# Pair 8 of an attention block sums its exponentials on VectorE too, and a weight conversion and one tile's transposes move forward

## The chip, the cores and the metric

The kernel runs on one core of a Trainium2 chip. The metric is the device time of one execution in microseconds (us); the runs of the kernel before have a median of 508.8 us (508.6 to 509.04). The engines are named as in the profile: PE is TensorE (matmuls), DVE is VectorE, ACT is ScalarE, POOL is GpSimd, SP is the engine that issues the transfers. Lines such as L415 are lines of the kernel before unless said otherwise.

## The reference, cut to what matters

All arrays are float32 but for the weights, which are float64.

```
attn:  s = (q @ k.T) / 8 ; s = 30 * tanh(s / 30) ; p = exp(s - max)      # 2 batches, 12 heads, 448 x 64
       out = (p / (sum(p) + 1e-9)) @ v
x   =  out laid out as 896 tokens x 768
moe:   h = x @ w_in                     # 768 -> 1024
       e = exp(h - max) ; solu = h * e / (sum(e) + 1e-9)
       ln = (solu - mean) / sqrt(var + 1e-6) * g_ln
       y = ln @ w_out                   # 1024 -> 768
moe2:  (sigmoid(y @ w_gate) * (y @ w_val)) @ w_out        # 768 -> 1536 -> 768
```

## The kernel before, in words

Four stages follow each other, and PE, ACT, DVE and POOL each run their instructions in the order in which the code issues them (a manual order holds for those four up to the end of the second matrix product; SP's transfers and what follows are placed by the scheduler).

**Attention.** The 24 heads are 12 pairs. A pair takes two slots (u = 0 and 1), each with half of the keys. In slot s, `s_mm` (L192) multiplies the scores of the next half on PE, `s_tanh` (L198) and `s_exp` (L220) work on ACT, and `s_pv` multiplies the exponentials of this slot with v (L238) and with a column of ones to get the row sums. For most pairs the sums come from the exponentials themselves: four matmuls in each of the two slots (L246). For the pairs in `ADD_PAIRS`, DVE first adds the two key blocks of each head (`es`, L232), in either slot, and four matmuls (L244) at the end of the second slot read the four added tiles. Pair 8 is in slots 16 and 17, pair 9 in 18 and 19. From slot 16 on the first matrix product (L405) of the first two token tiles is worked in beside attention: at the end of slot 16 `x_split` cuts tile 0 of x into a high and a low part (ACT L391, DVE `xl` L392), and at the end of slot 17 the first 12 of that tile's 36 matmuls stand.

**First product, tiles 2 to 6.** Tokens are in seven tiles of 128. A loop over t runs the 36 matmuls of tile t, then the transposes of tile t - 1 (`ln_trans`, L449, 8 on PE). On DVE stand `ln_max` (L415, after the tile's last matmul), `ln_he` (L423, after ACT's exponential L420), `ln_stats` (L429 to L434, then POOL L435), `ln_evac` of tile t - 1 (ACT L455 writes `lnhi`, then DVE L456 writes `lnlo`) and the first line of `ln_norm` (L439), after which ACT normalises the tile (L441).

**Weight conversion.** The float64 weights of the second product come as 12 chunks, two for each of its six column blocks. A chunk has six steps, which are in a list `todo`: A on ACT (L347), B, C and D on DVE (L352, L353, L354), E on DVE and ACT (L355, L334, then the cast L336 that gives the high part), F on DVE (L339, the low part). `fill(n)` issues the next n steps of the list where it stands in the code. The chunks overlap in the list: from chunk 3 on each group of six reads F of chunk c - 2, E of c - 1, B, C, D of c, A of c + 1. Five steps are issued in attention; before, the loop over t issues four for each of five tiles, 20 in all.

**Second product.** `l2(m, g)` makes column block m for token group g (tiles 0 to 2, or 3 to 6): 24 matmuls (L634) into one of two PSUM buffers (`pso`, tag `o`), then the evacuation of the block before (`y_evac`: ACT L648 writes `y_hi`, DVE L649 writes `y_lo`), then `fill(4)`. The order is (0, 0), (1, 0), the transposes and evacuation of tile 6, then (0, 1), (1, 1) and the rest. The third block, (0, 1), writes the PSUM buffer of the first, and reads the parts of tile 6. Third and fourth product follow.

Of the kernel before, what the change touches and what calls it, by code (L numbers as in the profile page):

```python
# [43 lines left out]
AHEAD = 3  # L44
W2_BUFS = 9

ADD_PAIRS = range(9, 11)

L1_BESIDE = 2
S_L1 = 16  # L50
# [22 lines left out]
def f32(ap):  # L73
    return ap.bitcast(F32)
# [7 lines left out]
def fused_kernel(ctx: ExitStack, tc: tile.TileContext, qk, v, cap, w_in, w_mid, g_ln, w_gv, w_fin, outT):  # L82
# [53 lines left out]
    with tc.If(bounded > 0) as cmp:  # L136
        network(tc, sh, False, w_in, w_mid, w_gv, w_fin, outT)
    with cmp.Else():
        network(tc, sh, True, w_in, w_mid, w_gv, w_fin, outT)
# [3 lines left out]
def network(ctx: ExitStack, tc: tile.TileContext, sh, general, w_in, w_mid, w_gv, w_fin, outT):  # L143
# [5 lines left out]
    def big():  # L149
        t = ps.tile([P, 2, 512], F32, tag="big", name="big")  # L150
        return t
# [70 lines left out]
    def s_pv(i, u):  # L222
# [4 lines left out]
        e = [es.pop((2 * i + j, u)) for j in range(2)]  # L227
        add = i in ADD_PAIRS and not general
        if add:
# [74 lines left out]
    def fill(k):  # L304
        for _ in range(min(k, len(todo))):
            todo.popleft()()
# [76 lines left out]
    def x_split(t, eng=nc.vector):  # L383
        xh = lin2.tile([P, K1, P], F32R, tag="xh", name="xh")
        xl = lin2.tile([P, K1, P], F32R, tag="xl", name="xl")
        t0 = t * P
        for b in range(B):
            lo, hi_ = max(t0, b * S), min(t0 + P, (b + 1) * S)
            if lo < hi_:
                src = x_sb[b][:, :, lo - b * S:hi_ - b * S]  # L390
                nc.scalar.copy(xh[:, :, lo - t0:hi_ - t0], src)  # L391
                eng.tensor_tensor(xl[:, :, lo - t0:hi_ - t0], src, f32(xh[:, :, lo - t0:hi_ - t0]), ALU.subtract)  # L392
        x_parts[t] = xh, xl

    def l1_mms(t):

        out = []

        def mm(half, kk, m):
            if t not in hts:  # L400
                hts[t] = big()
            xh, xl = x_parts[t]
            l, r = ((xh, wi_hi), (xh, wi_lo), (xl, wi_hi))[m]
            c = slice(half * 512, half * 512 + 512)
            nc.tensor.matmul(hts[t][:, half], l[:, kk], r[:, kk, c], start=(kk == 0 and m == 0), stop=(kk == K1 - 1 and m == 2))  # L405

        for half in range(2):
            for kk in range(K1):
                for m in range(3):
                    out.append(lambda half=half, kk=kk, m=m: mm(half, kk, m))  # L410
        return out

    def ln_max(t):
        sts[t] = lin2.tile([P, 24], F32, tag="st", name="st")
        nc.vector.tensor_reduce(sts[t][:, 0:1], hts[t].rearrange("p a b -> p (a b)"), AX.X, ALU.max, negate=True)  # L415

    def ln_exp(t):
        st = sts[t]
        lnes[t] = lin2.tile([P, F1], F32, tag="e", name="e", bufs=1)
        nc.scalar.activation(lnes[t], hts[t].rearrange("p a b -> p (a b)"), AF.Exp, bias=st[:, 0:1], accum_out=st[:, 1:2])  # L420

    def ln_he(t):
        nc.vector.tensor_tensor(lnes[t], hts.pop(t).rearrange("p a b -> p (a b)"), lnes[t], ALU.mult)  # L423

    def ln_stats(t):


        st, e = sts[t], lnes[t]
        nc.vector.tensor_scalar(st[:, 16:17], st[:, 1:2], EPS, None, ALU.add)  # L429
        nc.vector.bn_stats(st[:, 2:8], e[:, :512])  # L430
        nc.vector.tensor_scalar(st[:, 17:18], st[:, 16:17], st[:, 16:17], 1e-6, ALU.mult, ALU.mult)
        nc.vector.bn_stats(st[:, 8:14], e[:, 512:])
        nc.vector.bn_aggr(st[:, 14:16], st[:, 2:14])
        nc.vector.tensor_tensor(st[:, 18:19], st[:, 15:16], st[:, 17:18], ALU.add)  # L434
        nc.gpsimd.tensor_tensor(st[:, 19:20], st[:, 18:19], sh.mhalf, ALU.pow)  # L435

    def ln_norm(t, late=False):
        st, e = sts.pop(t), lnes[t]
        nc.vector.tensor_scalar(st[:, 20:21], st[:, 14:15], st[:, 19:20], -1.0, ALU.mult, ALU.mult)  # L439
        if late:  # L440
            nc.scalar.activation(e, e, AF.Identity, bias=st[:, 20:21], scale=st[:, 19:20])  # L441
        else:
            nc.gpsimd.tensor_scalar(e, e, st[:, 19:20], st[:, 20:21], ALU.mult, ALU.add)

    def ln_trans(t):
        e = lnes[t]
        lnes[t] = tp = big()
        for kk in range(K2):
            nc.tensor.transpose(tp[:, kk // 4, (kk % 4) * P:(kk % 4 + 1) * P], e[:, kk * P:(kk + 1) * P], ident)  # L449

    def ln_evac(t):
        g = 0 if t < 3 else 1
        c = slice(t * P - GROUPS[g][0], t * P - GROUPS[g][0] + P)
        tv = lnes.pop(t).rearrange("p a (k b) -> p (a k) b", b=P)
        nc.scalar.copy(ln_hi[g][:, :, c], tv)  # L455
        nc.vector.tensor_tensor(ln_lo[g][:, :, c], tv, f32(ln_hi[g][:, :, c]), ALU.subtract)  # L456
# [25 lines left out]
    def run(fs):  # L482
        while fs:
            fs.pop(0)()
# [36 lines left out]
    for s in range(-1, NS):  # L521
        m = s + 1
# [45 lines left out]
    t = L1_BESIDE  # L568
# [18 lines left out]
    for t in range(L1_BESIDE, 7):  # L587
        if t == 3:
            x0.close()
        if t == 2:  # L590
            lnt2 = lns.enter_context(tc.tile_pool(name="lnt2" + sfx, bufs=1, side="right", reuse_waits="tile"))
            ln_hi[1] = lnt2.tile([P, K2, NT - G1], F32R, name="lnhi1")
            ln_lo[1] = lnt2.tile([P, K2, NT - G1], F32R, name="lnlo1")
            w2p = lns.enter_context(tc.tile_pool(name="w2p" + sfx, bufs=W2_BUFS, side="right", reuse_waits="tile"))
        k = FILL_T if wide else 0
        if t > L1_BESIDE:
            mms = l1_mms(t)
            run(mms[:18])
        fill(k)
        run(mms[18:])  # L600
        if t > L1_BESIDE:
            ln_trans(t - 1)
        else:
            run(late[:1])
        ln_max(t)
        if t + 2 < 7:
            x_split(t + 2)
        ln_exp(t)
        if t == 6:
            ln_he(t)  # L610
            ln_stats(t)
            ln_evac(t - 1)
            ln_norm(t, True)
            fill(3 * k)
            continue
        fill(k)
        ln_he(t)
        ln_stats(t)
        if t > L1_BESIDE:
            ln_evac(t - 1)  # L620
        else:
            run(late[1:])
        ln_norm(t, True)
        fill(2 * k)
    wi.close()
    ytp = ctx.enter_context(tc.tile_pool(name="ytp" + sfx, bufs=1, side="left", reuse_waits="tile"))
    y_hi = ytp.tile([P, K3, NT], F32R, name="y_hi")
# [3 lines left out]
    def prod(out, w, kw, xh, xl, kx, first, last):  # L631
        wh, wl = w[kw // 4][:, 0, kw % 4], w[kw // 4][:, 1, kw % 4]
        for m, (l, r) in enumerate(((wh, xh), (wh, xl), (wl, xh))):
            nc.tensor.matmul(out, l, r[kx], start=(first and m == 0), stop=(last and m == 2))  # L634

    def l2(m, g):
        while len(w2[m]) < 2:
            fill(1)
        t0, t1 = GROUPS[g]
        n = t1 - t0  # L640
        o = pso.tile([P, 512], F32, tag="o", name="l2o")
        for kk in range(K2):
            prod(o[:, :n], w2[m], kk, ln_hi[g], ln_lo[g], (slice(None), kk), kk == 0, kk == K2 - 1)
        run(y_evac)
        fill(FILL_2 if wide else 0)

        def evac():
            nc.scalar.copy(y_hi[:, m, t0:t1], o[:, :n])  # L648
            nc.vector.tensor_tensor(y_lo[:, m, t0:t1], o[:, :n], f32(y_hi[:, m, t0:t1]), ALU.subtract)  # L649

        y_evac.append(evac)

    y_evac = []
    l2(0, 0)
    l2(1, 0)
    ln_trans(6)
    ln_evac(6)
    for m in range(2):
        l2(m, 1)
    for m in range(2, K3):  # L660
# [96 lines left out]
```

## Time and profile before

| what | value |
|---|---|
| median of 3 runs | 508.8 us |
| the profiled execution's own time | 508.99 us |
| its span, first to last instruction | 507.2 us |
| PE busy | 493.2 us (97%) |
| DVE busy | 332.5 us (66%) |
| ACT busy | 245.6 us (48%) |
| mean granted PE clock | 0.996 of full |

The span is what the trace shows; 1.8 us of the execution lie around it. [...] A matmul's duration overlaps with the next one's, so that PE's pace is read from starts. An engine's start times in the rows say when an instruction began; the bracket at the end of a row says how long the engine had stood idle before and who ended that.

### The profile page before, as it was taken

Reading aid. Unit: us, or ns where it says so; the run is one execution under the profiler, and the core shown is the slowest. Engines: PE = TensorE matmul, PEld = TensorE weight load, DVE = VectorE, ACT = ScalarE, POOL = GpSimd, SP = SyncE. Lnnn points to the kernel's source line nnn. Section 1 sums busy time; section 2 is a strip of 40 time slices with the busy share of each in tenths; the row PEclk is TensorE's granted clock in tenths of the full one; section 3 lists DMA queues with packets and bytes.
Section 4 is the critical chain, followed back from the end, with each engine's and each line's share of the span. In section 5 each row is a group of like instructions: output and inputs, shape, how many; then the busy total and the mean of one; then the engine's idle time right before and its main releaser. Section 6 shows DMA issues by size and latency. Waiting matters only on the chain.

```text
span 507.2 us, 6531 instructions
## 1 busy us (share of the span) xinstructions
PE 493.2 (97%) x2480; PEld 385.4 (76%) x2480; DVE 332.5 (66%) x571; ACT 245.6 (48%) x338; POOL 50.0 (10%) x38
## 2 busy tenths in 40 slices
PE   8999999999999969999999999999999999999995
PEld 4333333554688857998999999999999999999995
DVE  0776853273789794789989888888787777551000
ACT  5999999675354542344464444433433443221000
POOL 0000101011200000000001211111111101000000
PEclk9999999999999998999999999999999999999999
DMA  7666755010101121234553544444333443511001
GB/s 242 202 213 176 229 167 165 19 38 19 48 14 41 43 83 43 83 124 156 176 165 127 172 126 125 126 122 121 92 105 95 125 124 102 160 37 38 19 36 41
DMA packets 19059, 55.05 MB, mean 109 GB/s; under 512 B 3212, under 2 KB 6156, under 8 KB 19020
## 3 DMA queue, kind: packets, MB, share of 16 engines
q1 hardware_dynamic: 19020, 54.56, 35.0%
q8 instruction: 21, 0.34, 0.3%
q14 instruction: 18, 0.15, 0.1%
HBM read 51.68 MB, written 2.79 MB: 107 GB/s over the span
## 4 chain that ended last, share of the span: by engine, by line
PE 82%; ACT 13%; DVE 3%; issue 1%; POOL 0%; ACTq 0%; POOLq 0%
PE big L634 34%; PE l4o L634 17%; PE l2o L634 11%; PE big L405 10%; ACT e L198 5%; ACT e L220 5%; PE big L192 3%; PE o L238 3%; ACT wi_hi L336 1%; PE big L449 1%; PE sums L246 1%; PE warm L125 1%; ACT to L254 1%; DVE st L415 0%; DVE e L423 0%
## 5 line engine op out<-in xcount | busy, mean ns | idle before, releaser
L634 PE MATMUL big<-y_hi,w_hl 128*128 128x448 f32 x576 | 161.8, 362 | 0.0
L634 PEld LDWEIGHTS big<-y_hi,w_hl 128*128 128x128 f32 x576 | 107.9, 187 | 8.0
L634 PE MATMUL big<-y_lo,w_hl 128*128 128x448 f32 x288 | 104.6, 363 | 0.0
L634 PE MATMUL l4o<-p_hi,w_hl 128*128 128x448 f32 x288 | 80.7, 361 | 0.0
L336 ACT CAST w_hl<-cvt 128x512 fp32r<-128x512 f32 x66 | 40.7, 617 | 68.2 <-PE big L634 41.8
L355 DVE SCALAR_TENSOR_TENSOR cvt<-w_raw,cvt 128x512 uint32<-128x512 uint32 x78 | 71.5, 919 | 1.3
L347 ACT ACTIVATE cvt<-w_raw 128x512 f32<-128x512 f32 x66 | 44.2, 670 | 55.9 <-DVE w_hl L339 34.4
L339 DVE TENSOR_TENSOR w_hl<-cvt,w_hl 128x512 fp32r<-128x512 f32 x66 | 47.1, 714 | 25.1 <-ACT w_hl L336 24.8
L634 PE MATMUL l2o<-lnhi,w_hl 128*128 128x384 f32 (+1 forms) x192 | 56.5, 373 | 4.1 <-DVE w_hl L339 3.0
L354 DVE SCALAR_TENSOR_TENSOR cvt<-w_raw,cvt 128x512 uint32<-128x512 uint32 x78 | 56.0, 719 | 1.4
L634 PEld LDWEIGHTS l4o<-p_hi,w_hl 128*128 128x128 f32 x288 | 54.0, 187 | 3.9
L634 PEld LDWEIGHTS big<-y_lo,w_hl 128*128 128x128 f32 x288 | 54.1, 188 | 3.0
L198 ACT ACTIVATE e<-big,cap_inv 112x896 f32<-112x896 f32 x48 | 46.6, 1039 | 14.0 <-PE big L192 14.0
L634 PE MATMUL l4o<-p_lo,w_hl 128*128 128x448 f32 x144 | 52.3, 363 | 0.0
L706 POOL TENSOR_TENSOR p_lo<-sg,p_hi 128x896 fp32r<-128x896 f32 x12 | 29.5, 2456 | 209.5 <-ACT p_hi L705 209.5
L220 ACT ACTIVATE e<-e,cap_abs 112x896 f32<-112x896 f32 x48 | 48.1, 1074 | 0.0
L352 DVE TENSOR_SCALAR cvt<-cvt 128x512 f32<-128x512 f32 x78 | 32.7, 419 | 20.8 <-ACT cvt L347 20.8
L238 PE MATMUL o<-e,v 112*64 112x448 f32 x192 | 43.4, 552 | 0.4 <-ACT to L254 0.3
L192 PE MATMUL big<-qk_raw 64*112 64x448 f32 x192 | 43.0, 559 | 0.3 <-ACT e L198 0.3
L634 PEld LDWEIGHTS l2o<-lnhi,w_hl 128*128 128x128 f32 x192 | 36.2, 192 | 9.3 <-DVE w_hl L339 3.6
L634 PE MATMUL l2o<-lnlo,w_hl 128*128 128x384 f32 (+1 forms) x96 | 35.7, 372 | 0.8 <-DVE lnlo L456 0.8
L192 PEld LDWEIGHTS big<-qk_raw 64*112 64x112 f32 x192 | 15.6, 172 | 26.4 <-issue 19.3
(80 smaller groups left out, 505.2 us busy)
## 6 DMA issues: line engine op xcount, KB each, us to landing
w_raw<-in_w_gv SPq DMA_DIRECT2D x36, 512.0 KB, 3.5
w_raw<-in_w_fin SPq DMA_DIRECT2D x18, 512.0 KB, 3.6
w_raw<-in_w_in SPq DMA_DIRECT2D x12, 512.0 KB, 4.8
w_raw<-in_w_mid SPq DMA_DIRECT2D x12, 512.0 KB, 3.7
qk_raw<-in_qk SPq DMA_DIRECT2D x12, 448.0 KB, 4.7
v<-in_v SPq DMA_DIRECT2D x12, 224.0 KB, 4.3
out_t<-ob SPq DMA_DIRECT2D x12, 224.0 KB, 2.3
qk_raw<-rd SPq DMA_DIRECT2D x22, 112.0 KB, 3.2
```

Source lines behind the costliest of these rows:

```text
L192: nc.tensor.matmul(sc[j][:KC, c, :S], r[d, 1, kc * KC:(kc + 1) * KC], r[d, 0], start=True, stop=True)
L198: nc.scalar.activation(e, es[n, u][:KC, :, :S], AF.Tanh, scale=sh.cap_inv[:KC])
L220: nc.scalar.activation(es[n, u], es[n, u], AF.Exp, scale=sh.cap_abs[:KC])
L238: nc.tensor.matmul(o[d, :S], vs[i][:, kc, d], e[j][:, c], start=(kc == 0), stop=(kc == 3))
L336: nc.scalar.copy(st["hi"], w)
L339: v.tensor_tensor(st["lo"], st["w"], f32(st["hi"]), ALU.subtract)
L347: first = lambda t, lo, hi: nc.scalar.activation(f32(t), f32(hi), AF.Abs)
L352: word(lambda t, lo, hi: v.tensor_scalar(f32(t), f32(t), as_f32(W_MOST), as_f32(W_LEAST), ALU.min, ALU.max)),
L354: word(lambda t, lo, hi: v.scalar_tensor_tensor(t, hi, TOP, t, ALU.bitwise_and, ALU.bitwise_or)),
L355: word(lambda t, lo, hi: (v.scalar_tensor_tensor(t, lo, 29, t, ALU.logical_shift_right, ALU.bitwise_or), upper())),
L405: nc.tensor.matmul(hts[t][:, half], l[:, kk], r[:, kk, c], start=(kk == 0 and m == 0), stop=(kk == K1 - 1 and m == 2))
L634: nc.tensor.matmul(out, l, r[kx], start=(first and m == 0), stop=(last and m == 2))
```

## The change

Three edits. `ADD_PAIRS` begins at pair 8 rather than 9. In the loop over t, `fill` takes more steps: five for each of tiles 2 to 4, six for tiles 5 and 6 (two of them ahead of `ln_he`, three at the tile's end), so that 27 steps rather than 20 stand ahead of the second product. And `l2` takes a function that it calls after its twelfth matmul; by that, tile 6's transposes and evacuation are issued in the middle of block (1, 0) and not behind it.

```
-ADD_PAIRS = range(9, 11)
+ADD_PAIRS = range(8, 11)
...
         ln_exp(t)
         if t == 6:
+            fill(2 * k)
             ln_he(t)
...
             fill(3 * k)
             continue
-        fill(k)
+        fill(k if t + 2 < 7 else 2 * k)
         ln_he(t)
...
         ln_norm(t, True)
-        fill(2 * k)
+        fill(3 * k)
...
-    def l2(m, g):
+    def l2(m, g, between=None):
...
             prod(o[:, :n], w2[m], kk, ln_hi[g], ln_lo[g], (slice(None), kk), kk == 0, kk == K2 - 1)
+            if between and kk == 3:
+                between()
...
     l2(0, 0)
-    l2(1, 0)
-    ln_trans(6)
-    ln_evac(6)
+    l2(1, 0, lambda: (ln_trans(6), ln_evac(6)))
```

On PE, in slots 16 and 17 (L238 is the product with v, L246 and L244 are the sums, L192 the scores of the next half):

```order
 L192 MATMUL big<-qk_raw 112x448 x4
 L238 MATMUL o<-e,v 64x448 x4
-L246 MATMUL sums<-e,ones 32x448 x4
 L192 MATMUL big<-qk_raw 112x448 x4
 L238 MATMUL o<-e,v 64x448 x4
-L246 MATMUL sums<-e,ones 32x448 x4
+L244 MATMUL sums<-es,ones 32x448 x4
 L405 MATMUL big<-wi_hi,xh 128x512
```

Four matmuls of slot 16 go; those of slot 17 read the added tiles. On DVE, in the same two slots (`xl` is the low part of tile 0 of x, `ts` the copy of the sums):

```order
 L264 SCALAR_TENSOR_TENSOR r<-r,guard 16x56
 L265 RECIPROCAL r<-r 16x56
+L232 TENSOR_TENSOR es<-e 112x448 x2
 L392 TENSOR_TENSOR xl<-x_158,xh 128x768
+L232 TENSOR_TENSOR es<-e 112x448 x2
 L253 COPY ts<-sums 128x448
 L264 SCALAR_TENSOR_TENSOR r<-r,guard 16x56
```

The additions of the first slot stand ahead of `xl`, those of the second behind it. On DVE, between the last statistic of tile 4 (L439) and the maximum of tile 5 (L415), before:

```order
L439 TENSOR_SCALAR st<-st 128x1
L339 TENSOR_TENSOR w_hl<-cvt,w_hl 128x512
L355 SCALAR_TENSOR_TENSOR cvt<-w_raw,cvt 128x512
L334 TENSOR_TENSOR cvt<-cvt,g_sb 128x512
L415 TENSOR_REDUCE st<-big 128x1
```

and now, in this place and, with the same rows, between tiles 5 and 6:

```order
L439 TENSOR_SCALAR st<-st 128x1
L355 SCALAR_TENSOR_TENSOR cvt<-w_raw,cvt 128x512
L334 TENSOR_TENSOR cvt<-cvt,g_sb 128x512
L352 TENSOR_SCALAR cvt<-cvt 128x512
L353 TENSOR_SCALAR cvt<-cvt 128x512
L354 SCALAR_TENSOR_TENSOR cvt<-w_raw,cvt 128x512
L415 TENSOR_REDUCE st<-big 128x1
```

Three instructions ahead of the maximum became five. Between tiles 5 and 6 there were two before (L353 and L354). On DVE behind the last statistic of tile 6, before (L649 is `y_lo` of block (0, 0), L456 `lnlo` of tile 6; the row ahead of these is L334):

```order
L352 TENSOR_SCALAR cvt<-cvt 128x512
L353 TENSOR_SCALAR cvt<-cvt 128x512
L354 SCALAR_TENSOR_TENSOR cvt<-w_raw,cvt 128x512
L339 TENSOR_TENSOR w_hl<-cvt,w_hl 128x512
L649 TENSOR_TENSOR y_lo<-l2o,y_hi 128x384
L355 SCALAR_TENSOR_TENSOR cvt<-w_raw,cvt 128x512
L334 TENSOR_TENSOR cvt<-cvt,g_sb 128x512
L352 TENSOR_SCALAR cvt<-cvt 128x512
L353 TENSOR_SCALAR cvt<-cvt 128x512
L354 SCALAR_TENSOR_TENSOR cvt<-w_raw,cvt 128x512
L456 TENSOR_TENSOR lnlo_1191<-big,lnhi_1190 128x8x128
L649 TENSOR_TENSOR y_lo<-l2o,y_hi 128x384
```

and now, where L652 is the line of `y_lo`:

```order
L439 TENSOR_SCALAR st<-st 128x1
L355 SCALAR_TENSOR_TENSOR cvt<-w_raw,cvt 128x512
L334 TENSOR_TENSOR cvt<-cvt,g_sb 128x512
L352 TENSOR_SCALAR cvt<-cvt 128x512
L353 TENSOR_SCALAR cvt<-cvt 128x512
L354 SCALAR_TENSOR_TENSOR cvt<-w_raw,cvt 128x512
L339 TENSOR_TENSOR w_hl<-cvt,w_hl 128x512
L355 SCALAR_TENSOR_TENSOR cvt<-w_raw,cvt 128x512
L334 TENSOR_TENSOR cvt<-cvt,g_sb 128x512
L456 TENSOR_TENSOR lnlo_1195<-big,lnhi_1194 128x8x128
L652 TENSOR_TENSOR y_lo<-l2o,y_hi 128x384
```

Eight conversion instructions now stand between L439 and L456; and the first `y_lo`, which stood five instructions ahead of L456, stands behind it.

## Rows read from the trace of the kernel before

**Rows 1.** Windows: length, each engine's busy time (instructions), granted clock, DMA share, GB/s.
```profile
86.74:118.40 31.66, 31.66 (x152) 16.33 (x148) 15.03 (x30) 21.00 (x26) 4.82 (x5) 1.00 0.11 30
...
195.50:502.00 306.50, 306.50 (x1525) 284.55 (x1524) 206.02 (x328) 107.64 (x165) 29.47 (x12) 1.00 0.35 107
...
192.50:195.50 3.00, 3.00 (x8) 2.33 (x8) 1.51 (x3) 0.62 (x1) 0.00 (x0) 0.50 0.42 124
```

**Rows 2.** Timeline of PE around tile 6's transposes: start, duration, instruction, idle before.
```profile
175.68 0.42 PE L634 MATMUL l2o<-lnhi,w_hl 128*128 128x384 f32 x1
...
187.97 1.03 PE L449 MATMUL big<-ident,e 128*128 128x128 f32 x8
190.11 0.49 PE L634 MATMUL l2o<-lnhi,w_hl 128*128 128x512 f32 x1 [1.10 <-ACT lnhi L455]
191.37 0.50 PE L634 MATMUL l2o<-lnlo,w_hl 128*128 128x512 f32 x1 [0.77 <-DVE lnlo L456]
```

**Rows 3.** Waits of the whole execution: total us, times, longest.
```profile
PE l2o L634 <- DVE w_hl L339: 3.0, 2, 2.2
```

**Rows 4.** Timeline of PE in slot 17, pair 8's second half.
```profile
84.20 1.72 PE L238 MATMUL o<-e,v 112*64 112x448 f32 x8
85.85 0.96 PE L246 MATMUL sums<-e,ones 112*32 112x448 f32 x8
86.74 0.50 PE L405 MATMUL big<-wi_hi,xh 128*128 128x512 f32 x1
```

**Rows 5.** Timeline of DVE: tile 0's low part, and pair 9's first additions.
```profile
84.58 0.96 DVE L392 TENSOR_TENSOR xl<-x,xh 128x768 fp32r<-128x768 f32 x1 [4.80 <-ACT xh L391]
...
88.16 1.08 DVE L232 TENSOR_TENSOR es<-e 112x448 f32<-112x448 f32 x2
```

**Rows 6.** Timeline of ACT: the exponentials of pair 8's second half.
```profile
81.86 1.97 ACT L220 ACTIVATE e<-e,cap_abs 112x896 f32<-112x896 f32 x2
```

**Rows 7.** Timeline of DVE from tile 4's last statistic to `y_lo`.
```profile
163.73 0.20 DVE L439 TENSOR_SCALAR st<-st 128x1 f32<-128x1 f32 x1
...
166.03 1.22 DVE L415 TENSOR_REDUCE st<-big 128x1 f32<-128x1024 f32 x1 [0.17 <-PE big L405]
...
172.76 0.20 DVE L439 TENSOR_SCALAR st<-st 128x1 f32<-128x1 f32 x1
...
175.09 1.23 DVE L415 TENSOR_REDUCE st<-big 128x1 f32<-128x1024 f32 x1 [1.06 <-PE big L405]
177.67 1.23 DVE L423 TENSOR_TENSOR e<-big,e 128x1024 f32<-128x1024 f32 x1 [1.35 <-ACT e L420]
...
181.82 0.20 DVE L439 TENSOR_SCALAR st<-st 128x1 f32<-128x1 f32 x1
...
182.54 0.68 DVE L355 SCALAR_TENSOR_TENSOR cvt<-w_raw,cvt 128x512 uint32<-128x512 uint32 x1
183.26 0.69 DVE L334 TENSOR_TENSOR cvt<-cvt,g_sb 128x512 f32<-128x512 f32 x1
183.87 0.42 DVE L352 TENSOR_SCALAR cvt<-cvt 128x512 f32<-128x512 f32 x1
...
184.78 0.69 DVE L354 SCALAR_TENSOR_TENSOR cvt<-w_raw,cvt 128x512 uint32<-128x512 uint32 x1
185.39 0.68 DVE L339 TENSOR_TENSOR w_hl<-cvt,w_hl 128x512 fp32r<-128x512 f32 x1
...
190.09 1.23 DVE L456 TENSOR_TENSOR lnlo<-big,lnhi 128x1024 fp32r<-128x1024 f32 x1 [0.70 <-ACT lnhi L455]
191.23 0.55 DVE L649 TENSOR_TENSOR y_lo<-l2o,y_hi 128x384 fp32r<-128x384 f32 x1
```

**Rows 8.** Timeline of ACT: tile 6's normalisation, a cast, tile 6's high part.
```profile
182.06 1.24 ACT L441 ACTIVATE e<-e,st 128x1024 f32<-128x1024 f32 x1 [3.52 <-DVE st L439]
183.99 0.62 ACT L336 CAST w_hl<-cvt 128x512 fp32r<-128x512 f32 x1 [0.68 <-DVE cvt L334]
...
189.04 1.01 ACT L455 CAST lnhi<-big 128x1024 fp32r<-128x1024 f32 x1 [0.52 <-PE big L449]
```

## The prediction

> **What bounds the kernel now.** I read the page first: PE is busy nearly throughout, and the chain that ended last is mostly PE's. So a change is worth what it does to PE's gaps, or to the number of its matmuls. Next the windows [rows 1]: between 86.74 and 118.40, and from 195.50 to 502.00, PE is busy all the time. Whatever delays PE at 86.74 cannot be made up before 118.40, and from there to the second product the work hangs together in a chain that starts from PE's last attention matmuls; whatever is won or lost up to the start of block (0, 1) at 190 to 191 us stays to the end. Last the timelines of the two places that the change touches. In slot 17 the sums take PE from 85.85 to 86.74, 0.89 us, with no gap on either side [rows 4]. Around tile 6, PE waits 3.0 us for low parts of the weights in block (1, 0) [rows 3], then 1.10 and 0.77 us for tile 6's high and low part after its transposes [rows 2]. [...]
>
> **Pair 8: fewer matmuls, one wait.** Four sum matmuls of slot 16 go, which at slot 17's price is 0.89 us off PE. The scores of pair 9 and the product with v move up by that: the latter could start at 84.20 - 0.89 = 83.31 [rows 4]. But half of its four matmuls read the second head's exponentials, which ACT ends at 81.86 + 1.97 = 83.83 [rows 6]. They are two rounds of 0.82 us (84.20 to 85.85), so it ends at about 85.5, a gain of 0.35 and not 0.89. Then the sums need the second slot's additions. These stand on DVE behind `xl`, and `xl` starts only at 84.58, when ACT has written the high part, after DVE has idled 4.80 us [rows 5]; it ends at 85.5. Two additions take 1.08 us [rows 5], so the last is ready at 86.6, 2.8 us after its exponentials. The last sum matmul starts then; four in parallel take 0.89, one alone a little less (0.82, the round of L238), so L405 starts at 87.4 to 87.5 in place of 86.74: **0.7 us later**. Behind the waiting matmul on PE stand all of L405 and the scores of pair 9, on which ACT waits. The slot-16 additions cost nothing: they fall into DVE's 4.80 us. Bounds: at best the additions are never waited for, 0.35 us earlier; at worst L405 is 1.1 us later, with the additions as far apart as the 0.96 of `xl`, the nearest longer row. I take 0.7, built from the rows of the same operations.
>
> DVE's queue is what decides this. [...]
>
> **More steps ahead of the second product.** By block (1, 0) the low parts that it reads are made before tile 6's multiply, so the 3.0 us [rows 3] go. What is late next is tile 6 itself. I take times on the axis of before, without the 0.7. On DVE, instructions that follow each other start 0.72, 0.61, 0.45, 0.46 and 0.61 us after one another for L355, L334, L352, L353, L354 (182.54 to 185.39, the two middle ones 0.91 together) [rows 7]; L339 takes 0.60 so (0.68 less the same overlap of 0.08).
>
> - Tile 5's maximum: the five steps start 0.12 after L439 at 163.73 and take 2.85, so 166.70 in place of 166.03: 0.67 later [rows 7]. The step F ahead of the multiply is hidden: DVE waits there 1.35 us for ACT's exponential [rows 7].
> - Tile 6's maximum: L439 at 172.76 + 0.67, and 2.97 again, so 176.40 in place of 175.09: 1.31 later. Before, two steps stood here, and DVE idled 1.06 us [rows 7].
> - Tile 6's last statistic: 181.82 + 1.31 = 183.13. Its normalisation starts 0.24 later and takes 1.24 [rows 8], so the transposes can start at 184.6. PE comes to them after 36 matmuls from 175.68; at 0.201 us for 448 columns (306.5 us for 1525 [rows 1]), 0.172 for 384, that is 181.9. So PE waits some 2.7 us. The tile's end falls into a wait in place of cover.
> - Behind the statistic DVE has eight conversion instructions before `lnlo`: the last, L334, starts 0.12 + 0.72 + 0.61 + 0.45 + 0.46 + 0.61 + 0.60 + 0.72 = 4.29 later, at 187.42. Its cast follows 0.73 later (183.26 to 183.99 [rows 7, 8]), at 188.15, and on ACT that cast stands ahead of tile 6's high part. So the high part starts at 188.7 (0.62 less overlap), though the transposes are done by 185.7.
> - `lnlo` 1.05 after it (189.04 to 190.09), at 189.7, and `y_lo` of block (0, 0) 1.14 after that and 0.55 long [rows 7, 8]: 191.45.
>
> Block (0, 1) writes the PSUM buffer of (0, 0), so its first matmul has to wait for that `y_lo`. Before, `y_lo` had long been done. It starts at 191.5 and its second matmul at 191.7, where the second started at 191.37 [rows 2]: 0.3 us later. To this comes a little from tile 3, where a two-instruction step now stands between `xl` and the multiply; together **0.4 to 0.5 us later**. Bounds: if tile 6's evacuation stood free of the conversion, block (0, 1) would follow (1, 0) directly, at 184.6 + 1.03 + 12 x 0.172 = 187.7, 3.5 us earlier; at worst every hand-over costs its 0.04 once more and the steps do not overlap, 1.0 later. From 195.50 on PE has no gap [rows 1], and the conversions of later blocks are issued earlier than before, so nothing else is gained or lost there.
>
> **The clock.** Its 1.5 us hang on gaps. They come to 4.9 us before (3.0, 1.10, 0.77) and to 6.5 after (2.7 and, from 187.7 to 191.5, 3.8). I leave the cost unchanged. Ends: it does not fall, 1.5 less; it falls for twice as long, 1.5 more.
>
> **Sum.** 508.99 (507.2 of span and 1.8 around it) + 0.7 + 0.45 = 510.15 for an execution like the profiled one; that lies 0.2 above the median, so **510.0** beside 508.8.
>
> **Rivals.**
> 1. *Faster: tile 6's evacuation really lies under the second half of (1, 0).* Mechanism: DVE reaches L456 before PE ends that block. It decides at 187.7; each us by which `y_lo` comes before 191.4 is a us won. Price 3.5, less the 0.7: 506.0, and 504.5 if the clock stays up too. For it: the waits of [rows 2, 3] are the ones the change goes for. Against: eight instructions and a cast ahead of it in both queues, and 1.3 us of delay before. 10%.
> 2. *The clock costs less,* falling inside the long wait, where it costs nothing, or not at all: 508.5. For: one gap in place of several. Against: before, it fell after gaps of 2.2 us and less. 15%.
> 3. *The clock costs more:* it falls after the first gap, too, or stays down longer: 511.5. For: more idle time, in longer pieces. Against: after the first gap PE's work up to 187.7 has slack of 3.8 us, so a low clock there would cost nothing. [...] 13%.
> 4. *Pair 8 waits for nothing,* because `xl` or the additions are quicker than their rows: 510.0 - 0.7 - 0.35 = 508.95, no change. Against: the order of DVE, which is fixed. 10%.
>
> **How the numbers follow.** The forecast has 52%, with a range of its own from 509.3 to 511.0. A measurement of this kernel tells changes from about 0.2%, 1.0 us: slower is above 509.8, faster below 507.8. Of the forecast some 0.36 lies above 509.8, and rival 3 with its 0.13: slower 0.5. The rest of the forecast, 0.16, with rivals 2 and 4: same 0.4. Rival 1: faster 0.1. The range runs from rival 2 to rival 3: 508.3 to 511.6; left out are rival 1 and the tails.
>
> **What would show it.** In slot 17, L244 follows a gap on PE that DVE L232 ends, and L405 starts near 87.4. The wait for L339 in block (1, 0) is gone. With the 0.7 added, tile 6's transposes start near 185.3 after some 2.7 us of waiting for ACT L441, and block (0, 1) near 192.2 after 3.8 us of waiting, ended by the `y_lo` of DVE (L652) and not by L455 or L456. The forecast is wrong if block (0, 1) starts before 190 (rival 1), if L405 starts at or before 86.74 (rival 4), or if the span at clock 0.50 is not about 3 us (rivals 2 and 3).

## The result and the profile after

The changed kernel takes 512.8 us in the median of 9 runs, beside 508.8 for the kernel before; the ratio is 1.0076, with a 95% interval from 1.0066 to 1.0085. That is 3.9 us slower. The prediction had the sign and the two places of the loss right and the size wrong: it said 510.0, and 512.8 lies outside its range. The profiled execution took 511.57 us (span 509.7), 2.6 above before's; of the 9 it is one of the quicker ones. One run of the experiments, at 2150 us, is left out of all numbers below.

PE's timeline comes first, from the last sums of pair 7, which the change does not touch. The columns are start, duration, instruction, and the idle time before it with what ended it.

```profile
78.03 0.96 PE L246 MATMUL sums<-e,ones 112*32 112x448 f32 x8
...
86.17 1.55 PE L244 MATMUL sums<-es,ones 112*32 112x448 f32 x6
88.26 0.94 PE L244 MATMUL sums<-es,ones 112*32 112x448 f32 x2 [0.54 <-DVE es L232]
89.13 0.50 PE L405 MATMUL big<-wi_hi,xh 128*128 128x512 f32 x1
...
187.23 1.09 PE L449 MATMUL big<-ident,e 128*128 128x128 f32 x8 [2.31 <-ACT e L441]
...
194.03 0.79 PE L635 MATMUL l2o<-lnhi,w_hl 128*128 128x512 f32 x1 [3.61 <-DVE y_lo L652]
194.62 0.63 PE L635 MATMUL l2o<-lnlo,w_hl 128*128 128x512 f32 x1
```

The same sums stood here before, from the kernel before:

```profile
77.39 0.96 PE L246 MATMUL sums<-e,ones 112*32 112x448 f32 x8
```

The two executions are 0.64 us apart before the change begins to act, and this start differs from run to run of the same kernel (78.33 in another run of this one). Times across kernels are compared below after taking it off. So read, L405, the first product's first matmul, comes at 88.49 on the axis of before, 1.75 later than 86.74 [rows 4], and the second matmul of block (0, 1) at 193.98, 2.61 later than 191.37 [rows 2]. Of that, 1.75 is pair 8's and 0.86 comes around the second product. The waits around the second product answer to [rows 3]:

```profile
PE l2o L635 <- DVE y_lo L652: 3.6, 1, 3.6
PE big L449 <- ACT e L441: 2.3, 1, 2.3
```

The wait for L339 is gone, and two others are there in place of it. Last, what stands behind them. DVE in slot 17 and from the last conversion to `y_lo`, then GpSimd in slot 17, then ACT:

```profile
85.23 0.96 DVE L392 TENSOR_TENSOR xl<-x,xh 128x768 fp32r<-128x768 f32 x1 [3.85 <-ACT xh L391]
86.11 2.10 DVE L232 TENSOR_TENSOR es<-e 112x448 f32<-112x448 f32 x2
...
189.99 0.69 DVE L334 TENSOR_TENSOR cvt<-cvt,g_sb 128x512 f32<-128x512 f32 x1
192.28 1.23 DVE L456 TENSOR_TENSOR lnlo<-big,lnhi 128x1024 fp32r<-128x1024 f32 x1 [1.60 <-ACT lnhi L455]
193.43 0.55 DVE L652 TENSOR_TENSOR y_lo<-l2o,y_hi 128x384 fp32r<-128x384 f32 x1
```

```profile
86.22 1.50 POOL L273 TENSOR_TENSOR x<-to,qk_raw 128x448 f32<-128x448 f32 x1 [3.81 <-ACT e L198]
```

```profile
190.72 0.62 ACT L336 CAST w_hl<-cvt 128x512 fp32r<-128x512 f32 x1 [2.25 <-DVE cvt L334]
191.25 1.01 ACT L455 CAST lnhi<-big 128x1024 fp32r<-128x1024 f32 x1
```

DVE's rows from 189.99 on and ACT's two are the chain that the prediction worked out, step by step: the last conversion, its cast, tile 6's high part behind that cast, the low part, `y_lo`. The rows of slot 17 are not as it had them: two additions that take 1.08 us for pair 9 [rows 5] take 2.10 here, and GpSimd's multiply L273 starts 0.11 behind the first of them; that it is the cause, an experiment below shows. They end at 88.21, and PE's last two sums start right behind them. The windows answer to the clock in [rows 1] (length, PE's busy time and matmuls, granted clock, DMA share, GB/s):

```profile
193.50:196.50 3.00, 2.47 (x6) 0.50 0.00 0
196.50:510.00 313.50, 308.10 (x1532) 1.00 0.35 105
```

In this execution the stretch at 0.50 is as long as before's, about 3.4 us. It begins at about 193.45 (the mean clock is 0.95 from 193.0 to 193.5 and 0.50 behind), within the long wait, and up to 194.03 it costs nothing.

### The profile page after: what moved, and what is told of

Read it like the earlier page. It is cut to its first block, busy times and chain, and to the rows that moved or that the text cites. A ratio compares the mean times of both kernels' runs of the same rounds, so it can differ in the third digit from the quotient of the medians.

```text
span 509.7 us, 6522 instructions
## 1 busy us (share of the span) xinstructions
PE 494.3 (97%) x2472; PEld 385.9 (76%) x2472; DVE 335.1 (66%) x575; ACT 246.3 (48%) x338; POOL 52.4 (10%) x38
## 4 chain that ended last, share of the span: by engine, by line
PE 78%; ACT 14%; DVE 5%; issue 2%; POOL 0%; ACTq 0%; POOLq 0%
PE big L635 34%; PE l4o L635 17%; PE l2o L635 10%; PE big L405 9%; ACT e L198 6%; ACT e L220 5%; PE big L192 3%; PE o L238 2%; ACT wi_hi L336 1%; PE big L449 1%; PE warm L125 1%; DVE e L423 1%; DVE lnlo L456 1%; ACT to L254 1%; PE sums L244 1%
## 5 line engine op out<-in xcount | busy, mean ns | idle before, releaser
L355 DVE SCALAR_TENSOR_TENSOR cvt<-w_raw,cvt 128x512 uint32<-128x512 uint32 x78 | 71.5, 918 | 1.3
L339 DVE TENSOR_TENSOR w_hl<-cvt,w_hl 128x512 fp32r<-128x512 f32 x66 | 45.3, 686 | 28.2 <-ACT w_hl L336 27.8
L354 DVE SCALAR_TENSOR_TENSOR cvt<-w_raw,cvt 128x512 uint32<-128x512 uint32 x78 | 53.6, 687 | 1.5
L707 POOL TENSOR_TENSOR p_lo<-sg,p_hi 128x896 fp32r<-128x896 f32 x12 | 31.1, 2592 | 206.5 <-ACT p_hi L706 206.5
L352 DVE TENSOR_SCALAR cvt<-cvt 128x512 f32<-128x512 f32 x78 | 35.1, 451 | 19.1 <-ACT cvt L347 18.9
L238 PE MATMUL o<-e,v 112*64 112x448 f32 x192 | 44.0, 552 | 0.4 <-ACT to L254 0.3
L192 PE MATMUL big<-qk_raw 64*112 64x448 f32 x192 | 43.0, 559 | 0.3 <-ACT e L198 0.3
L353 DVE TENSOR_SCALAR cvt<-cvt 128x512 uint32<-128x512 uint32 x78 | 34.9, 449 | 1.7
L192 PEld LDWEIGHTS big<-qk_raw 64*112 64x112 f32 x192 | 15.6, 172 | 26.5 <-issue 20.1
```

The costliest lines, as they stand in the source:

```text
L192: nc.tensor.matmul(sc[j][:KC, c, :S], r[d, 1, kc * KC:(kc + 1) * KC], r[d, 0], start=True, stop=True)
L238: nc.tensor.matmul(o[d, :S], vs[i][:, kc, d], e[j][:, c], start=(kc == 0), stop=(kc == 3))
L339: v.tensor_tensor(st["lo"], st["w"], f32(st["hi"]), ALU.subtract)
L352: word(lambda t, lo, hi: v.tensor_scalar(f32(t), f32(t), as_f32(W_MOST), as_f32(W_LEAST), ALU.min, ALU.max)),
L354: word(lambda t, lo, hi: v.scalar_tensor_tensor(t, hi, TOP, t, ALU.bitwise_and, ALU.bitwise_or)),
L355: word(lambda t, lo, hi: (v.scalar_tensor_tensor(t, lo, 29, t, ALU.logical_shift_right, ALU.bitwise_or), upper())),
```

## The experiments

Each was timed in five rounds beside the kernel before; the ratios are to that. The first four take the change apart.

**Pair 8 alone.**

```
-ADD_PAIRS = range(9, 11)
+ADD_PAIRS = range(8, 11)
```

> Only ADD_PAIRS is changed; the loop's fills and the second product are those of the kernel before. Theory A (the additions of slot 17 stand on DVE behind xl and are stretched while POOL multiplies beside them; the trace of the changed kernel has 1.57 us for one of them, against 0.55 for others): L405 starts about 1.7 us later relative to the scores before it, nothing makes this up, and the time is 1.7 us above the kernel before, about 510.5. Theory B (pair 8 costs nothing in the end; the whole loss is made around the second product): 508.4 to 508.9. My prediction's figure for this edit was +0.7.

Measured: 510.07 us, ratio 1.0033 (1.0020 to 1.0046), which is 1.7 us. L405 starts 1.75 later, as in the whole change; the two additions take 2.11 us at 85.59, with L273 on GpSimd from 85.61 for 1.60. At L405 pair 8 costs more than twice the 0.7 predicted. That the time, too, comes out at 1.7 (1.0 to 2.3 by the interval) is in part luck. In the profiled execution, once its start is taken off, the second product starts 2.26 later, as another operation, L289, takes 0.97 us beside GpSimd in place of 0.23 (shown below); and the low stretch lies in block (1, 0), so that block (0, 1) runs at the full clock, which it did not before.

**The conversion steps alone** (the three `fill` lines of the change).

> Only the fills of the loop are changed, 27 steps ahead of the second product rather than 20; pair 8 and the place of tile 6's transposes are those of the kernel before. Theory A: the wait for L339 in block (1, 0) goes, but DVE comes to tiles 5 and 6 later and has the same steps ahead of lnhi and lnlo of tile 6, so that block (0, 1) starts about 1.4 us later than before: about 510.2 with the clock cost of before. Theory C (the steps fit into idle DVE time and cost nothing): the 3.0 us of waiting are saved, 505.8 to 507.

Measured: 511.19 us in the median of seven runs, ratio 1.0042 (1.0028 to 1.0056), which is 2.1 us. PE's waits:

```profile
PE l2o L635 <- ACT lnhi L455: 4.9, 1, 4.9
PE l2o L635 <- DVE lnlo L456: 1.0, 1, 1.0
```

The 3.0 us for L339 are gone here too, and PE waits 5.9 us for tile 6 in place of 1.9. With the start taken off, the second matmul of block (0, 1) comes 1.0 later than before. The expected mechanism holds; the low stretch is twice as long as before's, 6.8 us, and takes the rest.

**The transposes inside the block alone** (`between` and the call of `l2(1, 0, ...)`).

> Only tile 6's transposes and evacuation are moved into block (1, 0). Theory A: without the added steps lnlo and the first y_lo come early on DVE, the evacuation lies under the second half of the block, and block (0, 1) starts 2.8 us earlier: 506.0, or 504.5 if the clock does not fall. Theory D (the move itself makes the PSUM buffer of block (0, 0) late and costs time): 508.8 or more.

Measured: 506.41 us, ratio 0.9955 (0.9935 to 0.9975): this edit alone makes the kernel faster, by 2.3 us.

```profile
PE l2o L634 <- DVE w_hl L339: 2.2, 1, 2.2
```

```profile
188.49 1.23 DVE L456 TENSOR_TENSOR lnlo<-big,lnhi 128x1024 fp32r<-128x1024 f32 x1 [2.02 <-ACT lnhi L455]
...
190.24 0.50 PE L634 MATMUL l2o<-lnhi,w_hl 128*128 128x512 f32 x1 [0.73 <-DVE y_lo L651]
190.57 0.39 PE L634 MATMUL l2o<-lnlo,w_hl 128*128 128x512 f32 x1
```

Tile 6's evacuation lies under the second half of (1, 0): `lnlo` starts 1.0 us before PE ends that block. Block (0, 1) waits for the `y_lo` of (0, 0), as in the change, but 0.73 us and not 3.61. This is the mechanism of rival 1. Conversions stand in DVE's queue ahead of `lnlo` here too, but DVE is through with them early and idles 2.02 us. The second matmul of (0, 1) comes 1.25 earlier than before (190.57 less 0.45 of start, beside 191.37). The rest of this execution's gain is the clock: its low stretch lies in the first half of (1, 0), and none of the matmuls behind 190 is slow.

**Both of these, without pair 8.**

> Fills and move together, without pair 8: the changed kernel less its first edit. Theory A: the two work against each other, block (0, 1) starts 0.4 to 0.7 us later than before and PE waits 2.7 and 3.8 us; 509.4 with the clock cost of before, up to 511 if the clock stays low for longer. Theory B (all of the loss is here): 512 to 513, as the changed kernel.

Measured: 509.63 us, ratio 1.0019 (1.0006 to 1.0032). The waits are the change's (2.32 for L441, 3.60 for `y_lo`). The 12 runs fall into two groups: four at a mean clock of 0.998 take 508.2 to 508.8 us, eight at 0.992 or 0.993 take 509.4 to 511.5. The profiled one is of the second group, with a low stretch twice as long as before's 3.4 us:

```profile
191.50:198.20 6.70, 5.52 (x13) 0.50 0.17 53
```

Theory A holds. The parts alone, 1.7 and 1.0, make 2.7 of the 3.9 us. The next three ask why pair 8 costs so much.

**Pair 8 with `xl` behind the additions.**

```
+        if i == 8 and u == 1:
+            run(xl_parts)        # xl of tile 0, put off until here
```

> Pair 8's additions alone, with tile 0's lower part `xl` issued behind the two additions of slot 17 instead of ahead of them. Theory A: pair 8's cost comes from the order on DVE: the additions stood behind `xl`, which waits for ACT's `xh` (84.58 before), and so fell beside GpSimd's multiply L273 (1.57 us for the second, 0.55 alone). Issued ahead of `xl` they run at about 83.5 to 85, before that multiply; the four sum matmuls that are left end earlier and L405 starts 0.2 to 0.5 earlier than in the kernel before (counted from the last scores): 508.2 to 508.6 us. Theory B: the additions cost what they cost wherever they stand (they are released late by the exponentials, or what is behind them, `xl`, is late for L405 instead): 510 us, as with the order as it is.

Measured: 509.22 us, ratio 1.0006 (0.9996 to 1.0015): no difference from the kernel before. The cost is one of order, but theory A's gain does not come. DVE in slot 17 and at L296 (L289 of before, an operation on 112x8 numbers), then PE, then GpSimd:

```profile
83.18 0.63 DVE L237 TENSOR_TENSOR es<-e 112x448 f32<-112x448 f32 x1 [2.19 <-ACT e L225]
84.11 0.63 DVE L237 TENSOR_TENSOR es<-e 112x448 f32<-112x448 f32 x1 [0.30 <-ACT e L225]
84.83 0.96 DVE L399 TENSOR_TENSOR xl<-x,xh 128x768 fp32r<-128x768 f32 x1
...
132.09 0.97 DVE L296 SCALAR_TENSOR_TENSOR rq<-rq,guard 112x8 f32<-112x8 f32 x1
```

```profile
83.56 2.29 PE L245 MATMUL o<-e,v 112*64 112x448 f32 x8
85.78 0.96 PE L251 MATMUL sums<-es,ones 112*32 112x448 f32 x8
86.67 0.50 PE L416 MATMUL big<-wi_hi,xh 128*128 128x512 f32 x1
```

```profile
131.84 1.21 POOL L454 TENSOR_SCALAR e<-e,st 128x1024 f32<-128x1024 f32 x1 [0.43 <-PE big L291]
```

The additions run as soon as their exponentials are there, and the sums wait for nothing. But the product with v takes 2.29 where it took 1.72 [rows 4], waiting for the second head's exponentials, so that four matmuls fewer bring L405 only 0.31 forward (86.67 less 0.24 of start). That is the 0.35 of the prediction. It is lost again at 132: GpSimd's L454 (L443 of before) begins first, and DVE's small operation takes 0.97 in place of 0.23 and ends with it, at 133.06 and 133.05; its follower releases a transpose on PE, which comes 0.5 later. In the kernel before DVE began 0.06 us ahead of GpSimd. Of the eight profiles with pair 8's additions four show this, of the six without none; the whole change has it in one of its two profiles.

**Pair 8 with L273 of pair 6 on VectorE.**

```
-        nc.gpsimd.tensor_tensor(x_sb[b][:, hp], ...)
+        (nc.vector if i == 6 and not general else nc.gpsimd).tensor_tensor(x_sb[b][:, hp], ...)
```

> Pair 8's additions alone, with the multiply of pair 6 (L273), which GpSimd makes beside them, issued on VectorE. Theory A: the second addition's 1.57 us are 0.55 us of work and about 1 us of GpSimd's multiply beside it: without it both additions take 0.5 to 0.6 us, and L405 comes 0.7 later than in the kernel before instead of 1.75: 509.3 to 509.6 us, if the multiply, some 0.55 us on DVE, stands behind the additions. Theory B: the addition is long for a reason of its own (a wait inside it for the exponential, PSUM or the like): it stays at 1.5 us, and the time at 510.1 us or above.

Measured: 510.64 us, ratio 1.0038 (1.0024 to 1.0051). The trace bears theory A out:

```profile
85.74 1.16 DVE L232 TENSOR_TENSOR es<-e 112x448 f32<-112x448 f32 x2
...
89.17 0.55 DVE L273 TENSOR_TENSOR x<-to,qk_raw 128x448 f32<-128x448 f32 x1
```

The two additions take 1.16 and L405 comes 0.79 later, the 0.7 of the prediction. The time does not: only the quickest of its five runs, the profiled one at 509.86, is near the expected 509.3 to 509.6, and why the others are up to 1.4 above it, at the same mean clock, is open.

**The waiting eviction first.** The whole change, with `y_lo` ahead of tile 6's transposes and the steps at that place moved behind.

```
-            fill(3 * k)                              # at t = 6
...
-        fill(FILL_2 if wide else 0)
+        fill(BLOCK_FILLS.pop(0) if wide and BLOCK_FILLS else FILL_2 if wide else 0)
...
+    BLOCK_FILLS = [0, 8]
     l2(0, 0)
-    l2(1, 0, lambda: (ln_trans(6), ln_evac(6)))
+    l2(1, 0, lambda: (run(y_evac), ln_trans(6), ln_evac(6)))
```

> The whole change, but inside block (1,0) the waiting eviction and subtraction of block (0,0) are issued ahead of tile 6's transposes, and the conversion steps that stood ahead of tile 6's lower parts (the three of t = 6) are put behind the first product's blocks instead. Theory A: the first matmul of block (0,1) waits for `y_lo` L652 alone because it stands behind `lnlo` of tile 6 on DVE; taken ahead of them it is no longer the releaser, block (0,1) starts on tile 6's `lnhi` about 3 us earlier (about 190.5 to 191.5 with pair 8's offset), and the time is 509.5 to 510.5 us against 512.8 of the change; the rest above the kernel before is pair 8's 1.4. Theory B: the block waits for tile 6's chain anyway, and the eviction in front of it only moves the wait to the transposes: 512 to 513 us.

Measured: 508.35 us, ratio 0.9995 (0.9983 to 1.0006), by the ratios 4.1 us below the change, pair 8's cost still in it. The waits are

```profile
PE big L449 <- ACT e L441: 2.3, 1, 2.3
PE l2o L634 <- DVE y_lo L651: 0.9, 1, 0.9
```

and the 0.9 is that of block (1, 1); (0, 1) follows without one. The seven runs at a mean clock of 0.996 or more take 507.1 to 508.9 us, the four at 0.994 or 0.995 take 509.3 to 509.7. Theory A's mechanism held. It expected 509.5 to 510.5 us, and only the four runs at the lower clock are near that. The edit moves the eviction and three steps at once; what either is worth alone, no run shows.

**TensorE kept busy in the change.** The added matmuls are the only difference.

```
+    def keep_busy(o, n):
+        for _ in range(n):
+            nc.tensor.matmul(o[:, :384], w2[0][0][:, 0, 0], ln_hi[0][:, 0], start=True, stop=True)
...
+        if t == 6:
+            keep_busy(tp[:, 0], 10)
...
+    keep_busy(big()[:, 0], 16)                       # behind block (1, 0)
```

> The whole change, with matmuls that nobody reads put where TensorE waits: 10 of 128x384 (0.17 us each at the full clock) ahead of tile 6's transposes, which waited 2.31, and 16 ahead of block (0,1), which waited 3.61. They write PSUM that is not read, and end before the waits do. Theory A: the part of the loss that differs from run to run is the clock at 0.50 after those two waits; with TensorE busy in them it stays at 1.00, the waits end when they did, and the time is 510 to 510.8 us with a mean clock of 0.998 or more. Theory B: the clock is not what costs (the waits cost by themselves, and the low clock falls beside other waits): 512 to 513 us as the change. Theory C: the added matmuls stand in the way (they end later than the waits): above 513 us.

**The changed kernel again**, on the same chip in the same rounds.

> The changed kernel itself once more, for a second profile and its runs beside those of the kernel with TensorE kept busy. Theory A: its runs fall into groups by the mean clock: 510 to 511 us at 0.998, 512 to 513.8 us at 0.991 to 0.993, where the stretch at 0.50 is longer than the 3.5 us of its first profile. Theory B: the time does not go with the mean clock.

Measured: 510.3 us (510.15 to 510.77, mean clock 0.998 or 0.999) with TensorE busy, 512.55 us (511.89 to 514.1, mean clock 0.993 to 0.996) without. PE around the two waits, busy first (L447 are the added matmuls), then the changed kernel's second profile:

```profile
185.70 1.03 PE L447 MATMUL big<-lnhi,w_hl 128*128 128x384 f32 x5
187.31 1.09 PE L455 MATMUL big<-ident,e 128*128 128x128 f32 x8 [0.57 <-ACT e L441]
...
190.32 2.94 PE L447 MATMUL big<-lnhi,w_hl 128*128 128x384 f32 x16
194.10 0.50 PE L641 MATMUL l2o<-lnhi,w_hl 128*128 128x512 f32 x1 [0.84 <-DVE y_lo L658]
194.44 0.40 PE L641 MATMUL l2o<-lnlo,w_hl 128*128 128x512 f32 x1
```

```profile
195.02 0.79 PE L635 MATMUL l2o<-lnhi,w_hl 128*128 128x512 f32 x1 [3.60 <-DVE y_lo L652]
195.61 0.63 PE L635 MATMUL l2o<-lnlo,w_hl 128*128 128x512 f32 x1
```

The same waits end by the same instructions; from there one runs at the full clock (20 us at 1.00), the other does not:

```profile
184.00:204.00 20.00, 18.59 (x96) 1.00 0.24 80
```

```profile
194.00:200.50 6.50, 5.48 (x13) 0.51 0.17 50
200.50:202.00 1.50, 1.50 (x7) 0.84 0.35 134
```

In this second profile (514.1 us) the low stretch is about 6.8 us long, twice that of the first (511.57), and most of it lies on busy PE. Matmuls nobody reads, put in place of the idle time, were worth 2.2 us, and the low stretch goes with them; theory A held in its main point. The groups by clock are less clean than expected (511.89 at 0.996, 511.99 at 0.993). The second profile has a further delay that the first and the busy one lack, at L289, which takes 0.23 in the first and 0.25 in the busy one:

```profile
134.86 0.97 DVE L289 SCALAR_TENSOR_TENSOR rq<-rq,guard 112x8 f32<-112x8 f32 x1
```

Its second matmul of block (0, 1) comes 3.30 later than before, start taken off, and not 2.61: 0.7 more. Part of the 2.2 may be that. The low stretch begins at about 194.2 (0.66 from 194.0 to 194.5), within the second of two waits of PE, 2.32 and 3.60 us long, and from 179 to 205 us it is the only one.

**TensorE kept busy in the kernel before**, 10 and 3 matmuls ahead of the two that wait for L339, 4 ahead of block (0, 1), 3 ahead of its second matmul.

> The kernel before, with unread matmuls of 128x384 where TensorE waits in it (10 and 3 ahead of the matmuls that waited 2.15 and 0.85 for L339, 4 ahead of block (0,1), 3 ahead of its second matmul), to have the change without the clock on both sides. Theory A: the low stretch of the kernel before, 3.5 us at 0.50, costs it about 1.7 us: 506.8 to 507.3 us at a mean clock of 0.998 or more, so that the change with TensorE kept busy (510.3) stands 3.0 to 3.5 above it, and the clock's share of the 4 us is only what the change's low stretch is longer, 0.5 to 1. Theory B: that stretch costs the kernel before little: 508.2 to 508.7 us, and the clock's share of the change's 4 us is over 2.

Measured: 508.03 us, ratio 0.9983 (0.9974 to 0.9992), mean clock 0.997 to 0.999, between the two theories. So without the clock on either side the change costs 1.0034 / 0.9983 = 1.0051, or 2.6 us, and 1.3 of its 3.9 are left for the clock. Both intervals together make that uncertain by 0.8 us or more. Two rows of this run, the second matmul of (0, 1) and PE's last matmul:

```profile
191.57 0.50 PE L641 MATMUL l2o<-lnlo,w_hl 128*128 128x512 f32 x1 [0.23 <-DVE lnlo L456]
...
500.29 0.36 PE L641 MATMUL l4o<-p_hi,w_hl 128*128 128x448 f32 x1
```

PE's last matmul in the kernel before, in the change's two profiles and in the change with TensorE busy:

```profile
501.72 0.36 PE L634 MATMUL l4o<-p_hi,w_hl 128*128 128x448 f32 x1
...
504.24 0.36 PE L635 MATMUL l4o<-p_hi,w_hl 128*128 128x448 f32 x1
...
506.73 0.36 PE L635 MATMUL l4o<-p_hi,w_hl 128*128 128x448 f32 x1
...
503.01 0.36 PE L641 MATMUL l4o<-p_hi,w_hl 128*128 128x448 f32 x1
```

From the second matmul of (0, 1) to the last one PE takes 308.72 and 308.57 us with TensorE busy, 310.35 in the kernel before, 309.62 and 311.12 in the change. So the clock costs the kernel before 1.6 us, and the change 1.0 in its first profile and 2.5 in its second: 0.6 less, and 0.9 more.

**Parts put together.** The move with the eviction first; 23 conversion steps ahead of the second product, spread so that none stands between tile 6's statistics and its evacuation; pair 8 with `xl` behind.

```
+FILLS = {2: (1, 1, 3), 3: (1, 1, 3), 4: (1, 1, 2), 5: (1, 2, 2), 6: (1, 3, 0)}
...
+    l2(1, 0, lambda: (run(y_evac), ln_trans(6), ln_evac(6)))     # then 0 and 4 steps
```

> Parts put together: tile 6's transposes inside block (1,0) with the eviction of (0,0) ahead of them, the conversion steps spread so that none stands ahead of tile 6's normalization and casts, pair 8's additions with `xl` behind them. Theory A (the costs are those of the order on DVE and ACT, each in its place): 503.5 to 505 us, 4 to 5 below the kernel before, of which the move alone gave 2.3. Theory B (the gain of the move is used up: block (0,1) then waits for tile 6 whatever stands ahead): 506 to 507 us, as the move alone.

Measured: 504.39 us (503.03 to 504.96), ratio 0.9911 (0.9895 to 0.9927), 4.5 us faster than the kernel before. Of its waits in the second product one is left, and the clock stays at 1.00 (180 to 200 us):

```profile
PE big L461 <- ACT e L453: 1.4, 1, 1.4
```

**The same without pair 8.**

> The combined kernel without pair 8's additions, with all else as there. Theory A: pair 8, with `xl` behind the additions, brought L405 0.31 forward in both kernels that have it, and 0.3 of it reaches the end where L289 does not meet GpSimd's L443: 504.4 to 505 us here, 0 to 0.5 above the combined kernel's 504.4. Theory B: the pair's additions are worth nothing (the slot waits for ACT's exponentials): 504.4 us, no difference. Theory C: they still cost: 503.5 us or less here.

Measured: 504.15 us (502.88 to 504.24), ratio 0.9904 (0.9890 to 0.9917). Theory B: pair 8's additions, even in the better order, are worth nothing that can be measured (the two ratios are 0.0007 apart). Both kernels beat before and after.

## Why the prediction was wrong

The ledger: pair 8 1.75 and the second product 0.85, both read in traces, together the 2.6 us that the ratios give without the clock (1.8 to 3.4 by their intervals). Of the 3.9 that leaves 1.3 for the clock and for the delay at L289, which one of the change's two profiles has. The prediction had 0.7 for pair 8, 0.45 for the second product, no change of the clock's cost and no term for L289.

- *Pair 8: the step that failed is "two additions take 1.08 us".* They took 2.10, as GpSimd's multiply lay beside them. With that multiply gone they took 1.16 and L405 came 0.79 later; so the order, the waiting sums and the 0.35 off the product with v were right, and the duration was that of a row with nothing beside it. This term was 1.05 us too small. The upper bound, 1.1, fell too: it was taken from `xl`, which has no neighbour on GpSimd either. The row that says it stands in the trace of before, six microseconds behind the one I used: the next two additions, on DVE,

```profile
94.39 1.65 DVE L232 TENSOR_TENSOR es<-e 112x448 f32<-112x448 f32 x2 [4.82 <-ACT e L220]
```

and the multiply beside them, on GpSimd:

```profile
93.88 1.15 POOL L273 TENSOR_TENSOR x<-to,qk_raw 128x448 f32<-128x448 f32 x1 [7.11 <-DMA qk_raw<-rd]
```

  The same pair of forms, 0.57 longer.
- *The second product: mechanism right, 0.4 too small.* The wait for L339 went; tile 6's transposes waited 2.31 (predicted 2.7), block (0, 1) 3.61 (3.8), released by L652. The first matmul of (0, 1) stands at 191.64 on the axis of before without pair 8 (predicted 191.5). With TensorE busy on both sides its second matmul is 0.85 later: 192.02 (194.44 less 0.66 of start and 1.76 of pair 8) and 191.17 (191.57 less 0.40), within the bounds of -3.5 to 1.0. The 0.55 above the 0.3 that it worked out ahead of tile 3's share: the first matmul is 0.2 later, the second follows it by 0.34 and not 0.2, and the kernel before is there 0.2 earlier when TensorE is kept busy.
- *The clock: "I leave the cost unchanged" failed.* Its 1.5 us are half of the 3.00 us at 0.50 [rows 1]; in the kernel before it costs 1.6 (310.35 less 308.72). That it hangs on gaps the runs with TensorE kept busy bear out: their clock stays at 1.00 around the second product, from 184 to 204 us in the change and from 180 to 200 in the kernel before. In the first profile the low stretch is as long as before, and costs 0.6 less, as it begins in the long wait; that is rival 2 in small. In the second it is twice as long and costs 0.9 more, which is rival 3. The mean clocks put most other runs beside the second (0.991 to 0.993), but they do not tell the two apart well: the first profile has 0.994, the second 0.993. Rival 3 was priced at 1.5; the comparison of the busy kernels leaves 1.3, and no trace shows more than 0.9 of it as the clock's. Its argument against (there is slack behind the first gap) does not reach the second gap, and there the clock fell.
- *The delay at L289, no term of the sum.* It costs 0.7 us in the second profile of the change and is absent from the first. How many of the other runs have it, the record does not show.
- *Rival 1* is what the move does alone, 2.3 us faster, 1.25 of it at block (0, 1) in its profile. The added conversion steps took it away: they make tile 6 late, and the last of them stands on DVE and ACT right ahead of its evacuation. Both were predicted, the rows from 189.99 on show the second, and the run with the eviction first agrees.

What stays open: how the last 1.3 us divide; why the low stretch is some 3.4 us in one run of the same kernel and 6.8 in another; and why the two parts without pair 8, by their mean clock, escape the low stretch more often than the whole change (four of twelve runs at 0.998 there, one of fifteen here).

## What to carry to other kernels

Before a duration from one row goes into a sum, look at what GpSimd does in the new place: here DVE's additions beside a GpSimd multiply took 2.10 us, and 1.16 with the multiply gone. Taking work off PE was worth what its next wait left: four matmuls fewer gave 0.3 us where the exponentials were late. And of several edits for one wait, try each alone: here one of them, 2.3 us faster, was hidden by the one beside it.

## What the hardware showed

Where DVE's additions and GpSimd's multiply lay beside each other, one or both took longer than alone. In slot 17 the first addition begins at 86.11 and takes 0.62, and GpSimd's multiply begins at 86.22: the multiply takes 1.50, 0.35 more than its 1.15, and ends at 87.72; the second addition takes 1.57, where the shortest of these takes 0.55, and ends 0.49 after the multiply, at 88.21. At 94.39 in the kernel before, the pair of additions is 0.57 longer behind a multiply that began at 93.88. At L289 it is 0.97 in place of 0.23, and both engines end together. That one engine waits for the other there is my reading of these times; no row shows such a wait. New to me was how small the difference is at L289: DVE starts 0.06 us ahead of GpSimd in the profiles with 0.23 or 0.25 and 0.25 behind it in those with 0.97, and that makes 0.5 to 0.7 us, also between two executions of the same kernel.

Around the second product the stretches at the low clock were about 3.4 or about 6.8 us long in every profile that had one. No one wait tells where they come: one began within a wait of 2.15 us (the move alone), and with the eviction first a wait of 2.31, followed by one of 0.89, left the clock at 1.00.
